# Constant tables made behind the first piece of the decay on VectorE

## The chip, the cores and the metric

The kernel runs on one core of a Trainium2 chip. The metric is device time in microseconds of one launch; the median of the runs shown is used. Five in-order instruction streams matter here: PE (TensorE matmuls, with weight loads shown as PEld), DVE (VectorE), ACT (ScalarE), POOL (GpSimd) and SP (SyncE, which issues nearly all transfers of the stretch in question).

## The reference, cut to what matters

Three layers run one after the other on four batches of 576 tokens.

```python
# attention, 32 heads of 64: causal, with a decay bias from running sums of s
cum  = np.cumsum(np.maximum(s, 0.0), axis=-1)
bias = -(cum[:, :, :, None] - cum[:, :, None, :])
scores = np.where(causal, -1e9, scale * q @ k.T + np.minimum(bias, 0.0))
attn = softmax(scores); x = attn @ v
# gated layer: 512 -> 1024 -> 1024 -> 512
x = (((x @ w1) * (x @ w2)) @ w3) @ w_out
# soft mixture of experts, 32 slots
logits = x @ phi
slot_input = softmax(logits, axis=0).T @ x
slot_out   = relu(slot_input @ w1[e]) @ w2[e]
out = softmax(logits, axis=1) @ slot_out
```

## The kernel before

**Attention.** There are 40 items: for the first eight heads, tokens 0 to 319 (items 0 to 7) and tokens 320 to 575 (items 8 to 15) are items of their own, later heads are one item each. An item's scores (`att_scores`, line 359) are matmuls over 68 rows: 64 of q or k and 4 *decay rows*, which hold the running sum of s and its rounding remainder. So no score of an item can start before its decay rows are in its `raw` tile. DVE takes the maximum (362), ACT the exponential (367), POOL normalises (380), PE transposes (395 for whole tiles, 409 for the diagonal ones), ACT copies the transposed tiles out of PSUM (397, 411), and PE multiplies by v for a pair of heads (`x_ps`), after which ACT and DVE split the result in two parts (444, 445). Transposed tiles go through a PSUM pool named `tp` of two buffers, so a transpose has to wait until the transposed tile two before it was copied out.

**The decay.** `decay_rows` handles the running sums in two pieces of 320 and 256 columns: a clamp (150), a scan (153), a rounded copy (169), its remainder (170), and the two negated (ACT 171, DVE 172). Items 0 and 1 take their decay rows straight from these tiles: four small transfers on SP (322). All others take them from a buffer in DRAM, which three larger transfers on SP fill (176, 177) behind the four and behind two further fetches; item 2 reads it back first (324).

**Weights.** The weights of the gated layer come as 64-bit floats in halves of 128x512 words (`raw_w`, SP line 188, three buffers), and are turned into 32-bit floats by ACT (202) and DVE (205, 206, 209), then split by ACT (233) and POOL (234). These conversions run beside the attention.

**The constant tables.** `masks` (786) makes three small tables from the identity matrix: `rep` (789), `sel4` (791, a copy of rep) and `half` (794). `choice_rows` (957) makes `part` (two reductions on line 962, and line 965). rep is first used by `sum_rows`, sel4 and half in the third layer's steps, part in its last steps.

**What sets the order.** SP issues in the order of the code. The order on PE, DVE, ACT and POOL is set by a scheduler that places instructions by their data and by modelled times. So an instruction that is moved on one engine changes the places of others, on its own engine and on the rest.

Of the kernel before, what the change touches and what calls it, by code (L numbers as in the profile page):

```python
# [11 lines left out]
F32R = mybir.dt.float32r  # L12
# [4 lines left out]
ALU = mybir.AluOpType  # L17
# [30 lines left out]
def attn_glu_softmoe_kernel(  # L48
# [95 lines left out]
    def decay_rows():  # L144
        t0 = dec[0]
        ones = t0[:, 1]
        nc.gpsimd.memset(ones, 1.0)

        def steps(c0, c1):
            nc.vector.tensor_scalar(  # L150
                out=t0[:, 0, c0:c1], in0=t0[:, 0, c0:c1], scalar1=0.0, scalar2=8.0, op0=ALU.max, op1=ALU.mult
            )
            nc.vector.tensor_tensor_scan(
                out=t0[:, 2, c0:c1], data0=ones[:, c0:c1], data1=t0[:, 0, c0:c1],
                initial=t0[:, 2, c0 - 1 : c0] if c0 else 0.0, op0=ALU.mult, op1=ALU.add,
            )

# [6 lines left out]
        for c0, c1 in ((0, 320), (320, 512), (512, S)):  # L164
            if c0 < 512:
                steps(c0, c1 if c1 < 512 else S)
            cum = t0[:, 2, c0:c1]
            p0, p1 = (x[:, :, :, c0:c1] for x in rows) if c1 <= 512 else (rest[:, 0], rest[:, 1])
            nc.vector.tensor_copy(p0[:, 0, 1].bitcast(F32R), cum)
            nc.vector.tensor_tensor(out=p1[:, 0, 1].bitcast(F32R), in0=cum, in1=p0[:, 0, 1], op=ALU.subtract)  # L170
            nc.scalar.activation(out=p0[:, 1, 0], in_=p0[:, 0, 1], func=AF.Copy, scale=-1.0)
            nc.vector.tensor_scalar(out=p1[:, 1, 0], in0=p1[:, 0, 1], scalar1=-1.0, scalar2=None, op0=ALU.mult)

# [583 lines left out]
    with tc.tile_pool(name="att", bufs=1) as ap:  # L757
# [28 lines left out]
        def masks():  # L786

            rep = cp.tile([P, NS], F32, name="rep")
            nc.vector.tensor_reduce(out=rep, in_=ident.rearrange("p (r s) -> p s r", s=NS), axis=AX.X, op=ALU.add)
            sel4 = cp.tile([P, 4, NS], F32, name="sel4")  # L790
            nc.vector.tensor_copy(sel4, rep.unsqueeze(1).broadcast_to([P, 4, NS]))

            half = cp.tile([P, 1], F32, name="half")
            nc.vector.tensor_reduce(out=half, in_=ident[:, :64], axis=AX.X, op=ALU.add)
            return rep, sel4, half
# [162 lines left out]
    def choice_rows():  # L958
        cb = c_all.rearrange("p (b t) s -> p b t s", t=5)

        for k, m in enumerate((8, 16)):
            nc.vector.tensor_reduce(
                out=part[:, k, 0:1], in_=ident.rearrange("p (a r s) -> p a r s", r=2, s=m)[:, :, 1], axis=AX.XY, op=ALU.add
            )
        nc.vector.tensor_scalar(
# [175 lines left out]
```

## Time and profile before

| | us |
|---|---|
| runs | 547.64, 550.87, 552.92 |
| median | 550.87 |
| the profiled execution | 552.43 |
| its span, from first to last instruction | 550.7 |
| mean granted clock of TensorE | 0.993 |

| engine | busy us | share of the span |
|---|---|---|
| PE | 516.8 | 94% |
| DVE | 329.0 | 60% |
| ACT | 311.6 | 57% |
| POOL | 130.6 | 24% |

Busy time is the time in which at least one instruction of the engine was running. The chain that ended last is PE for 70% of the span, transfers for 13%, DVE for 8%. Shares over the whole span say little of one stage: between 200 and 480 us PE hardly ever stands still, and in the first 150 us it waits for a microsecond or less at a time, each time for something else.

### The profile page before, as it was taken

The page shows a single profiled execution, that of the slowest core. Times are in us where ns is not written, and L with a number is a line of the kernel's source. Part 1 is how long each engine was busy: PE and PEld are TensorE (multiplying, and loading weights), DVE is VectorE, ACT ScalarE, POOL GpSimd, SP SyncE. Part 2 cuts the span into 40 slices and gives each one's busy share as a digit, 9 for nine tenths or more (in the row PEclk, how much of TensorE's full clock was granted, in tenths as well). Part 3 has the DMA queues.
Part 4 walks back from the last instruction along what each step waited for, and adds up shares of the span by engine and source line. Part 5 has one row for each costly group of instructions (what it writes and reads, how often), then busy time and mean ns, then how long its engine had stood idle before and what let it go on. Part 6 is the DMA issues. An engine that isn't in the chain of part 4 may idle for free.

```text
span 550.7 us, 11764 instructions
## 1 busy us (share of the span) xinstructions
PE 516.8 (94%) x4288; PEld 434.3 (79%) x4288; DVE 329.0 (60%) x1016; ACT 311.6 (57%) x845; POOL 130.6 (24%) x199
## 2 busy tenths in 40 slices
PE   2799899998999999999999999999999999989993
PEld 2567678877788898999989889899989999843452
DVE  7558787879987394866577668566630311252433
ACT  4567667687986674866577567558644211321222
POOL 4475563102454232110221311111310000000000
PEclk9999989999999999999999999999999999999998
DMA  5746973977673253563656537553514999689977
GB/s 147 235 146 193 280 223 128 292 259 269 218 253 102 73 161 113 169 201 133 194 170 211 173 99 208 176 172 114 167 44 137 413 411 376 241 293 423 420 295 241
DMA packets 38809, 118.03 MB, mean 214 GB/s; under 512 B 4224, under 2 KB 10560, under 8 KB 35296
## 3 DMA queue, kind: packets, MB, share of 16 engines
q1 hardware_dynamic: 36768, 113.60, 61.0%
q10 hardware_dynamic: 1984, 3.69, 2.4%
q8 instruction: 34, 0.56, 0.4%
q14 instruction: 23, 0.19, 0.1%
HBM read 102.11 MB, written 11.60 MB: 206 GB/s over the span
## 4 chain that ended last, share of the span: by engine, by line
PE 70%; DMA 13%; DVE 8%; ACT 4%; issue 2%; POOL 1%; SPq 0%; ACTq 0%; DVEq 0%; POOLq 0%
PE gl L457 31%; PE sc_ps L359 7%; PE x_ps L110 7%; PE pt_ps L395 5%; DMA raw_w<-in_w 5%; PE gn_ps L627 3%; PE o_ps L1042 3%; DMA raw_w3t<-in_w3t 3%; PE h_ps L1004 3%; PE ptd_ps L409 2%; PE z_ps L110 2%; DMA raw_wot<-in_wot 2%; DVE sc L362 1%; PE lg L110 1%; ACT sc L367 1%
## 5 line engine op out<-in xcount | busy, mean ns | idle before, releaser
L457 PE MATMUL gl<-x,w12t 128*128 128x320 f32 (+1 forms) x1536 | 237.7, 304 | 0.1
L457 PEld LDWEIGHTS gl<-x,w12t 128*128 128x128 f32 x1536 | 212.7, 190 | 7.4 <-issue 4.4
L380 POOL TENSOR_SCALAR sc<-sc,rinv 128x64 f32<-128x64 f32 (+4 forms) x160 | 101.1, 650 | 253.0 <-DVE rinv L377 85.7
L367 ACT ACTIVATE sc<-sc,nmax 128x64 f32<-128x64 f32 (+4 forms) x160 | 89.8, 563 | 31.4 <-DVE nmax L362 29.1
L362 DVE CUSTOM_DVE_ANT_0 sc<-sc_ps,mask 128x64 f32<-128x64 f32 (+4 forms) x160 | 65.0, 423 | 31.8 <-PE sc_ps L359 31.0
L397 ACT COPY pt<-pt_ps 128x128 f32<-128x128 f32 (+3 forms) x128 | 53.0, 426 | 34.1 <-PE pt_ps L395 25.1
L395 PE MATMUL pt_ps<-ident,sc 128*128 128x128 f32 x320 | 56.6, 286 | 5.5 <-POOL sc L380 3.2
L395 PEld LDWEIGHTS pt_ps<-ident,sc 128*128 128x128 f32 x320 | 38.4, 144 | 16.9 <-POOL sc L380 7.2
L463 ACT COPY a<-gl 128x256 f32<-128x256 f32 (+1 forms) x64 | 25.4, 398 | 46.0 <-PE gl L457 40.7
L359 PE MATMUL sc_ps<-qa 128*128 128x64 f32 (+1 forms) x144 | 46.4, 334 | 1.3 <-DVE gT L475 0.8
L110 PE MATMUL x_ps<-pt,v 128*64 128x256 f32 (+1 forms) x384 | 47.4, 358 | 0.0
L359 PE MATMUL sc_ps<-raw 68*128 68x288 f32 (+4 forms) x96 | 35.8, 516 | 11.6 <-DMA raw<-rows 9.8
L359 PE MATMUL sc_ps<-qb 68*128 68x64 f32 (+1 forms) x144 | 43.6, 306 | 0.9 <-DMA qb<-qa 0.9
L110 PEld LDWEIGHTS x_ps<-pt,v 128*64 128x64 f32 x384 | 33.5, 140 | 5.8 <-issue 1.0
L359 PEld LDWEIGHTS sc_ps<-raw 68*128 68x128 f32 x96 | 21.6, 265 | 16.9 <-issue 14.1
L202 ACT ACTIVATE w_w<-raw_w 128x512 f32<-128x512 f32 x32 | 21.6, 676 | 17.8 <-DMA raw_w<-in_w 17.7
L445 DVE TENSOR_TENSOR x<-x_ps,x 128x320 fp32r<-128x320 f32 (+1 forms) x32 | 14.1, 452 | 29.2 <-ACT x L444 29.2
L630 ACT COPY gn<-gn_ps 128x512 f32<-128x512 f32 x40 | 22.5, 584 | 15.5 <-PE gn_ps L627 15.1
L367 ACT ACTIVATION_READ_ACCUMULATOR sc<-sc,nmax 128x1 f32 x160 | 30.9, 193 | 0.0
L359 PEld LDWEIGHTS sc_ps<-qa 128*128 128x128 f32 x144 | 27.4, 190 | 3.6 <-DVE gT L475 1.3
L409 PE MATMUL ptd_ps<-ident,sc 128*128 128x128 f32 x160 | 25.9, 286 | 3.2 <-ACT pt L397 3.0
L359 PEld LDWEIGHTS sc_ps<-qb 68*128 68x128 f32 x144 | 27.4, 191 | 1.6 <-DVE v_sb L276 1.0
(180 smaller groups left out, 725.6 us busy)
## 6 DMA issues: line engine op xcount, KB each, us to landing
ew<-in_ew SPq DMA_DIRECT2D x27, 1024.0 KB
raw_w<-in_w SPq DMA_DIRECT2D x32, 512.0 KB
raw<-in_qk SPq DMA_DIRECT2D x24, 576.0 KB
v<-in_v SPq DMA_DIRECT2D x16, 576.0 KB
raw_w3t<-in_w3t SPq DMA_DIRECT2D x16, 512.0 KB
raw_wot<-in_wot SPq DMA_DIRECT2D x8, 512.0 KB
raw_wo<-in_wo SPq DMA_DIRECT2D x8, 512.0 KB
w_d<-w_w SPq DMA_DIRECT2D x8, 512.0 KB
```

Source lines behind the costliest of these rows:

```text
L110: mm = nc.tensor.matmul(out_, lhs, rhs, start=start, stop=stop)
L202: line_up(nc.scalar.activation(out=w, in_=hi.bitcast(F32), func=AF.Copy, scale=F64_SCALE))
L359: nc.tensor.matmul(pp[:r, : z - a], x[:, 0, q0 : q0 + r], x[:, 1, a:z], start=x is mul[0], stop=x is mul[-1])
L362: nc.vector.tensor_tensor_reduce(out=sc[:r, a:z], in0=pp[:r, : z - a], in1=hd["mask"][:r, m0 : m0 + z - a], scale=-0.125, scalar=3.0e38 if ...
L367: nc.scalar.activation(out=sc[:r, :W], in_=sc[:r, :W], func=AF.Exp, bias=nmax[:r, i : i + 1], scale=-1.0, accum_out=rsum[:r, i, 0:1],)
L380: nc.gpsimd.tensor_scalar(out=sc, in0=sc, scalar1=rinv[:, i : i + 1], scalar2=1.0, op0=ALU.mult, op1=ALU.mult)
L395: nc.tensor.transpose(tp[:, j * P : (j + 1) * P], sc[:, j * P : (j + 1) * P], ident)
L397: t["turned", i] = nc.scalar.copy(out=pt[:, p0 : p0 + step * (i - 1) + 1 : step], in_=tp[:, : i * P].rearrange("p (j q) -> p j q", q=P))
L409: nc.tensor.transpose(dg[:, p0 : p0 + P], t["sc"][:, c0 : c0 + P], ident)
L457: nc.tensor.matmul(acc[:, :nt], w12_t[fc][:, wi, n, kc], x_t[b, blk, kc][:, xi], start=k == 0, stop=k == 3 * KC - 1)
L463: st["a_copy"] = nc.scalar.copy(out=a_sb[:, :nt], in_=acc[:, :nt])
L630: st["turned", blk, k, h] = nc.scalar.copy(out=gn[:r, 4 * h : 4 * h + 4].rearrange("p c f -> p (c f)"), in_=tp[:r])
```

## The change

The first instruction of each table on DVE (`rep`, `half`, and the two reductions of `part`) is told to stand behind the last DVE pass of the first piece of the decay (the negation of its remainder, line 172 before, 180 now). It is an order on the same engine, with no semaphore of its own. sel4 and line 965 follow as readers of these. The helper `line`, which wraps the decay passes, only keeps the last step in a list; its loop does nothing.

```diff
+        order = mybir.DependencyInfo(mybir.DependencyClass.NoSync, mybir.DependencyReason.DATA)
+        seq = []
+
+        def line(step):
+            for p in seq:
+                pass
+            seq[:] = [step]
...
-            nc.vector.tensor_scalar(out=p1[:, 1, 0], in0=p1[:, 0, 1], scalar1=-1.0, scalar2=None, op0=ALU.mult)
+            line(nc.vector.tensor_scalar(out=p1[:, 1, 0], in0=p1[:, 0, 1], scalar1=-1.0, scalar2=None, op0=ALU.mult))
+            if not c0:
+                hd["first"] = seq[0]
+
+    def after_first(step):
+        order = mybir.DependencyInfo(mybir.DependencyClass.NoSync, mybir.DependencyReason.DATA)
+        tc.add_manual_dep(step.ins, hd["first"].ins.name, order, reason="order")
...
-            nc.vector.tensor_reduce(out=rep, in_=ident.rearrange("p (r s) -> p s r", s=NS), axis=AX.X, op=ALU.add)
+            after_first(nc.vector.tensor_reduce(out=rep, in_=ident.rearrange("p (r s) -> p s r", s=NS), axis=AX.X, op=ALU.add))
...
-            nc.vector.tensor_reduce(out=half, in_=ident[:, :64], axis=AX.X, op=ALU.add)
+            after_first(nc.vector.tensor_reduce(out=half, in_=ident[:, :64], axis=AX.X, op=ALU.add))
...
-            nc.vector.tensor_reduce(
+            after_first(nc.vector.tensor_reduce(
                 out=part[:, k, 0:1], in_=ident.rearrange("p (a r s) -> p a r s", r=2, s=m)[:, :, 1], axis=AX.XY, op=ALU.add
-            )
+            ))
```

No instruction is added or removed. In the changed kernel, lines of `decay_rows` stand 8 further down and lines behind it 14 further down (359 is 373, 397 is 411, and so on).

DVE at the start of the program, before, from the second clamp of the decay to the pass ahead of line 172 (`dec` is the decay's work tile, `rows_128` and `rows_129` are the tiles that the four small transfers read, `w_w_0_0` is the first half of the weights):

```order
L150 TENSOR_SCALAR dec<-dec 32x256
L789 TENSOR_REDUCE rep<-ident 128x32
L153 SCALAR_TENSOR_TENSOR dec<-dec 32x320
L794 TENSOR_REDUCE half<-ident 128x1
L962 TENSOR_REDUCE part<-ident 128x1 x2
L791 COPY sel_626<-rep 128x128
L169 CAST rows_128<-dec 32x320
L153 SCALAR_TENSOR_TENSOR dec<-dec 32x256
L965 TENSOR_SCALAR part<-part 128x2
L170 TENSOR_TENSOR rows_129<-dec,rows_128 32x320
L169 CAST rows_128<-dec 32x192
L169 CAST rows_130<-dec 32x64
```

The next two rows are a pass over `w_w_0_0` (205) and then line 172 for `rows_129`. The same stretch now:

```order
L158 TENSOR_SCALAR dec<-dec 32x256
L161 SCALAR_TENSOR_TENSOR dec<-dec 32x320
L177 CAST rows_128<-dec 32x320
L161 SCALAR_TENSOR_TENSOR dec<-dec 32x256
L178 TENSOR_TENSOR rows_129<-dec,rows_128 32x320
L177 CAST rows_128<-dec 32x192
L177 CAST rows_130<-dec 32x64
L180 TENSOR_SCALAR rows_129<-rows_129 32x320
L803 TENSOR_REDUCE rep<-ident 128x32
L808 TENSOR_REDUCE half<-ident 128x1
L178 TENSOR_TENSOR rows_129<-dec,rows_128 32x192
```

Six table instructions and the weight pass have gone from ahead of the negation to behind it.

ACT, some 50 instructions in, before (items 4 to 8; `pt_4`, `ptd_4` are the transposed tiles of item 4, `x_0_0_1` is the product with v of items 2 and 3, `w_w12_3_0` and `w_w12_3_1` are the halves of the weight tile 3):

```order
L397 COPY pt_3_369<-pt_ps_3_2_374 128x2x128
L411 COPY ptd_3_370<-ptd_ps_3_378 128x192
L367 ACTIVATE sc_6_453,rsum_1_94<-sc_6_453,nmax_7_515 128x320
L202 ACTIVATE w_w12_3_0_553<-raw_w12_3_0_390 128x512
L397 COPY pt_4_428<-pt_ps_4_1_430 128x128
L444 CAST x_0_0_1_157<-x_ps_2_0_392 128x320
L397 COPY pt_4_428<-pt_ps_4_2_443 128x2x128
L202 ACTIVATE w_w12_3_1_602<-raw_w12_3_1_441 128x512
L367 ACTIVATE sc_8_563,rsum_2_95<-sc_8_563,nmax_8_562 128x448
L411 COPY ptd_4_429<-ptd_ps_4_447 128x192
```

And now:

```order
L216 ACTIVATE w_w12_3_0_553<-raw_w12_3_0_390 128x512
L411 COPY pt_3_369<-pt_ps_3_2_374 128x2x128
L381 ACTIVATE sc_6_453,rsum_1_94<-sc_6_453,nmax_7_515 128x320
L425 COPY ptd_3_370<-ptd_ps_3_378 128x192
L216 ACTIVATE w_w12_3_1_602<-raw_w12_3_1_441 128x512
L247 CAST w12t_3_552<-w_w12_3_0_553 128x512
L381 ACTIVATE sc_8_563,rsum_2_95<-sc_8_563,nmax_8_562 128x448
L381 ACTIVATE sc_8_563,rsum_2_95<-sc_8_563,nmax_8_562 128x576
L247 CAST w12t_3_552<-w_w12_3_1_602 128x512
L411 COPY pt_4_428<-pt_ps_4_1_430 128x128
L458 CAST x_0_0_1_157<-x_ps_2_0_392 128x320
L411 COPY pt_4_428<-pt_ps_4_2_443 128x2x128
```

Both halves of the weight tile 3 and both exponentials of item 8 now stand ahead of the copies of item 4's transposed tiles and of the split of x.

PE at the same place, before:

```order
L359 MATMUL sc_ps_7_2_0_534<-raw_7_312 128x320
L395 MATMUL pt_ps_3_2_374<-ident_86,sc_2_235 128x128 x2
L409 MATMUL ptd_ps_3_378<-ident_86,sc_2_235 128x128 x3
L110 MATMUL x_ps_2_0_392<-ptd_2_329,v_3_250 64x64
L395 MATMUL pt_ps_4_1_430<-ident_86,sc_4_343 128x128
L110 MATMUL x_ps_2_0_392<-ptd_3_370,v_3_250 64x64
```

And now:

```order
L373 MATMUL sc_ps_7_2_0_534<-raw_7_312 128x320
L409 MATMUL pt_ps_3_2_374<-ident_86,sc_2_235 128x128 x2
L423 MATMUL ptd_ps_3_378<-ident_86,sc_2_235 128x128 x3
L373 MATMUL sc_ps_8_3_0_564<-raw_8_362 128x448
L373 MATMUL sc_ps_8_4_0_574<-raw_8_362 128x288
L373 MATMUL sc_ps_8_4_1_577<-raw_8_362 128x288
L409 MATMUL pt_ps_4_1_430<-ident_86,sc_4_343 128x128
L110 MATMUL x_ps_2_0_392<-ptd_2_329,v_3_250 64x64
L110 MATMUL x_ps_2_0_392<-ptd_3_370,v_3_250 64x64
```

Item 8's scores, which stood behind this x_ps and the next transposes, now stand ahead of it. Earlier on PE, the three diagonal transposes of item 0 (409, `ptd_ps`) have moved from ahead of item 2's scores to behind them. Behind the first quarter of the program, PE, POOL and SP stand as before.

## Rows read from the trace of the kernel before

**Rows 1.** Busy time by stretch: PE, PEld, DVE, ACT, POOL, clock, transfer share, GB/s.
```profile
20.00:30.00 10.00, 10.00 (x31) 7.72 (x31) 5.09 (x25) 4.85 (x17) 5.11 (x8) 1.00 0.89 257
...
72.00:90.00 18.00, 16.81 (x97) 14.03 (x93) 16.40 (x37) 15.05 (x34) 10.41 (x8) 0.91 0.56 179
...
200.00:480.00 280.00, 279.62 (x2348) 258.27 (x2348) 151.61 (x480) 155.89 (x430) 47.54 (x85) 1.00 0.58 194
```

**Rows 2.** Chain that ended last, 40 to 64 us: start, length, engine, tile, line.
```profile
39.97 0.43 PE pt_ps L395 x2
...
43.96 0.62 PE pt_ps L395 x2
...
55.86 7.06 DMA raw_w<-in_w
```

**Rows 3.** Chain that ended last, first 20 us.
```profile
4.11 0.28 DVE rep L789
...
5.12 0.11 DVE half L794
5.23 0.26 DVE part L962 x2
5.49 0.13 DVE sel L791
...
6.51 0.06 DVE part L965
...
6.97 0.27 DVE rows L169 x2
...
7.50 0.31 DVE rows L172
```

**Rows 4.** Timeline of SP, first 10 us: start, length, queue, line, transfer, count.
```profile
6.45 3.39 SPq L322 DMA_DIRECT2D raw<-rows  x4
...
7.88 0.65 SPq L322 DMA_DIRECT2D raw<-rows  x1
```

**Rows 5.** Timeline, first 32 us; in brackets idle before, and what ended it.
```profile
9.79 4.61 PE L359 MATMUL sc_ps<-raw 68*128 68x64 f32 x12 [9.79 <-DMA raw<-rows]
...
11.30 0.83 SPq L176 DMA_DIRECT2D rows_d<-rows  x2
...
17.79 0.90 PE L409 MATMUL ptd_ps<-ident,sc 128*128 128x128 f32 x3 [1.28 <-ACT pt L397]
```

**Rows 6.** Share of the transfer engines in tenths, 0 to 10 us, 40 slices.
```profile
DMA  0000000849798998976997868753321100000000
```

**Rows 7.** Timeline of PE, 30 to 60 us.
```profile
31.93 0.37 PE L110 MATMUL x_ps<-ptd,v 128*64 128x64 f32 x1 [0.85 <-ACT ptd L411]
...
44.37 2.10 PE L359 MATMUL sc_ps<-raw 68*128 68x448 f32 x6
...
47.52 1.96 PE L359 MATMUL sc_ps<-raw 68*128 68x448 f32 x6 [0.61 <-DVE w_w L205]
```

**Rows 8.** Share of the transfer engines in tenths, 30 to 50 us, 40 slices.
```profile
DMA  0000000000478379696986986420027777899999
```

**Rows 9.** Timeline of ACT, 36 to 70 us.
```profile
44.88 0.68 ACT L202 ACTIVATE w_w<-raw_w 128x512 f32<-128x512 f32 x1
...
47.13 0.26 ACT L397 COPY pt<-pt_ps 128x128 f32<-128x128 f32 x1
47.29 0.63 ACT L233 CAST w12t<-w_w 128x512 fp32r<-128x512 f32 x1
```

**Rows 10.** Timeline of DVE, 36 to 70 us.
```profile
46.09 0.69 DVE L209 SCALAR_TENSOR_TENSOR w_w<-raw_w,w_w 128x512 uint32<-128x512 uint32 x1
46.69 0.45 DVE L362 CUSTOM_DVE_ANT_0 sc<-sc_ps,mask 128x288 f32<-128x288 f32 x1
...
48.57 1.65 DVE L209 SCALAR_TENSOR_TENSOR w_w<-raw_w,w_w 128x512 uint32<-128x512 uint32 x1
```

**Rows 11.** Timeline of SP, 36 to 110 us.
```profile
45.97 0.52 SPq L188 DMA_DIRECT2D raw_w<-in_w  x1
```

More of the change, by code (lines that the diff above doesn't have):

```diff
@@ L147, in decay_rows @@
         nc.gpsimd.memset(ones, 1.0)
+        order = mybir.DependencyInfo(mybir.DependencyClass.NoSync, mybir.DependencyReason.DATA)
[4 more added lines that the diff above has]
+            seq[:] = [step]
         def steps(c0, c1):
-            nc.vector.tensor_scalar(
+            line(nc.vector.tensor_scalar(
                 out=t0[:, 0, c0:c1], in0=t0[:, 0, c0:c1], scalar1=0.0, scalar2=8.0, op0=ALU.max, op1=ALU.mult
-            )
-            nc.vector.tensor_tensor_scan(
+            ))
+            line(nc.vector.tensor_tensor_scan(
                 out=t0[:, 2, c0:c1], data0=ones[:, c0:c1], data1=t0[:, 0, c0:c1],
                 initial=t0[:, 2, c0 - 1 : c0] if c0 else 0.0, op0=ALU.mult, op1=ALU.add,
-            )
+            ))
         rows = [wp.tile([NH, 2, 2, 512], F32, tag="W", name=f"rows_{a}", bufs=NW) for a in range(2)]
@@ L168, in decay_rows @@
             p0, p1 = (x[:, :, :, c0:c1] for x in rows) if c1 <= 512 else (rest[:, 0], rest[:, 1])
-            nc.vector.tensor_copy(p0[:, 0, 1].bitcast(F32R), cum)
-            nc.vector.tensor_tensor(out=p1[:, 0, 1].bitcast(F32R), in0=cum, in1=p0[:, 0, 1], op=ALU.subtract)
+            line(nc.vector.tensor_copy(p0[:, 0, 1].bitcast(F32R), cum))
+            line(nc.vector.tensor_tensor(out=p1[:, 0, 1].bitcast(F32R), in0=cum, in1=p0[:, 0, 1], op=ALU.subtract))
             nc.scalar.activation(out=p0[:, 1, 0], in_=p0[:, 0, 1], func=AF.Copy, scale=-1.0)
-            nc.vector.tensor_scalar(out=p1[:, 1, 0], in0=p1[:, 0, 1], scalar1=-1.0, scalar2=None, op0=ALU.mult)
+            line(nc.vector.tensor_scalar(out=p1[:, 1, 0], in0=p1[:, 0, 1], scalar1=-1.0, scalar2=None, op0=ALU.mult))
[4 more added lines that the diff above has]
+        tc.add_manual_dep(step.ins, hd["first"].ins.name, order, reason="order")
     def decay_store():
@@ L961, in choice_rows @@
         for k, m in enumerate((8, 16)):
-            nc.vector.tensor_reduce(
+            after_first(nc.vector.tensor_reduce(
                 out=part[:, k, 0:1], in_=ident.rearrange("p (a r s) -> p a r s", r=2, s=m)[:, :, 1], axis=AX.XY, op=ALU.add
-            )
+            ))
         nc.vector.tensor_scalar(
```

## The prediction, made before the changed kernel ran

> **What bounds the kernel now.** I read the busy time by stretches first: it shows which engine has no slack, and where. From 200 to 480 us PE is busy for 279.62 of 280 us [rows 1]. Its work there is fixed, so whatever PE gains or loses before 200 us arrives at the end nearly one for one, as long as nothing after it starts to wait. The question is then what the change does to PE's waits in the first stage. The chain of waits shows that stage as one of many short links: the decay passes on DVE until the first scores, PE afterwards, and from 55.86 us on the fetches of the weights [rows 2]. The timeline of PE shows its holes one by one, and the share of the transfer engines tells when a fetch must have landed.
>
> The table instructions lie on the chain. Between the second clamp of the decay and the negation of the first remainder (line 172) it counts rep 0.28, half 0.11, part 0.26, sel4 0.13 and line 965 0.06, in sum 0.84 us; and from the end of the copies of line 169 at 6.97 + 0.27 = 7.24 to line 172 at 7.50 there are 0.26 us more, for the weight pass that also moves [rows 3]. What waits for line 172 is the second of the four small transfers: line 172 ends at 7.81, the transfer is issued at 7.88, and SP is then busy with issuing up to 9.84 [rows 4]. The first scores start at 9.79, when the decay rows have come [rows 5].
>
> **The change, part by part.** *The front.* All of 0.84 + 0.26 = 1.10 us goes from ahead of line 172. Against it stands one pair of passes, the scan and its copy, that now follow each other directly; I take 0.05 for it, about the size of the smallest piece above. So line 172 should end 1.05 us sooner, at 6.76, the second small transfer be issued at 6.83 and the first scores start at 8.74. Behind the second small transfer SP issues without a gap, so the store to DRAM that is now issued at 11.30 [rows 5] also moves by 1.05, to 10.25. Its other condition, the last negation, is met earlier: even with tables and the weight pass in front of it, everything on DVE up to there is the same set of passes as before. Item 2 and all that follow hang on this store. The instructions that were moved cost nothing where they go: DVE passes the same work before the store is issued, and the tables' first readers come much later.
>
> The small transfers could gain less. The transfer engines are busy with the first weights and the first q and k until about 8.0 us (the 32nd of 40 slices is the last with a share) [rows 6]. If the rows only move after that, they land as long after 8.0 as now after the issue's end, 9.79 - 8.53 = 1.26, so at 9.3, and the first scores gain 0.5. [...] I take 1.05 for the chain as a whole, since the store is bound by SP's issuing and not by this landing; 0.5 is kept as the end of the range.
>
> *The diagonal transposes of item 0.* They took 0.90 us in a hole that PE had anyway, from 17.79 [rows 5]. Now they stand behind item 2's scores, in a stretch where PE is busy for 10.00 of 10 us [rows 1]. That would be 0.90 lost, but the same stretch ends in a wait of 0.85 us for ACT at 31.93 [rows 7], which is as long, so I take 0.05 and keep 0.90 as the bound. To here PE is 1.0 us ahead.
>
> *The order at 39 to 52 us.* This is the term that decides. Before, PE ends item 7's scores at 39.97 and needs until 43.96 + 0.62 = 44.58 for the transposes of item 3, x_ps and the transposes of item 4 [rows 2]; item 8's scores then take it to 44.37 + 2.10 = 46.47 [rows 7]. Now item 8's scores come first. PE starts at 38.97, has 4.61 + 1.89 = 6.50 us of work, and arrives at item 4's diagonal transposes at 45.5. These need a buffer of `tp`, so the copy of item 4's first tile by ACT. That copy now stands behind both conversions of the weight tile 3. The second half's words have landed when the transfer engines fall silent, at about 43.2 (slices of 0.5 us from 30 on) [rows 8], so now at about 42.2. From there: ACT's pass 0.68 [rows 9]; on DVE two passes of the maximum and three of the conversion, which took from 46.69 to 48.57 + 1.65 = 50.22, so 3.53 us, or 2.57 if the last of them takes 0.69 as it did at 46.09 [rows 10]; then the split and the copy on ACT, 47.13 to 47.92, so 0.79 [rows 9]. The copy ends at 42.2 + 0.68 + 0.79 + 2.57 to 3.53, at 46.2 to 47.2. PE waits 0.7 to 1.7 us; the long pass is the exception among the two shown, so I take 1.2, and allow 2.1, since the next transposes wait for the next copies. Against it the wait of 0.61 before item 9's scores [rows 7] goes, since item 8's maxima are long done by then. The net loss is 0.6, between 0.1 and 1.5.
>
> *The rest.* Up to about 100 us some instructions change places by one or two; I set these at nothing: instructions that swap with a neighbour delay one what they bring forward for the other, and PE, POOL and SP keep their order soon after. The cover for it is thin (from 72 to 90 us DVE is busy for 16.40 of 18 us, ACT for 15.05 [rows 1]); if it fails, the price is that of the second rival.
>
> **The sum.** -1.05 + 0.05 + 0.6 = -0.4 us against the profiled execution of 552.43, whose span is 550.7. That gives 552.0 there. The median of the runs is 550.87, 1.56 below the profiled execution, so the forecast in the measure of the median is **550.5 us**. With all ends in its favour the sum is -1.05 + 0.1 = -0.95; with all against it, -0.5 + 0.9 + 1.5 = +1.9.
>
> **The rivals.**
> *The gain arrives whole.* If the words of weight tile 3 land a microsecond or two sooner than the silence of the transfer engines tells (it only gives the latest time), or PE makes up the new hole from the next ones, -1.0 remains: 549.9 us. For it speaks that one fetch need not be the last to land; against it, that the conversion on DVE alone is 2.57 us at best.
> *The weights come late.* The mechanism that ends slower: SP issues in the order of the code, and the fetch of v, which waits for the buffer that x_ps frees, stands ahead of the next weight fetch at 45.97 [rows 11]. PE now ends that x_ps at 45.5 - 0.62 = 44.9 instead of 43.96, so this fetch goes out 0.9 later. Its words are wanted by ACT in front of item 9's last exponential, and the fetches that follow are on the chain, the first with 7.06 us [rows 2]. If the delay of 0.9 is passed on and ACT stands still for as long once more, PE loses 0.9 + 0.9 on top of the forecast: 552.3 us. It decides from the point where the conversion of weight tile 4 waits for its words by more than 1 us. Against it: tile 3 is converted earlier than before, so ACT and DVE have room when the words come.
> *The front gains little.* The small rows stay behind the first weights, and the store too lands no earlier: the order at 39 to 52 us then costs its 0.6 without a gain, 551.5 us.
> [...]
>
> **How the numbers follow.** Forecast 0.38, gain whole 0.25, weights late 0.20, front gains little 0.08, clock 0.09. One per cent of 550.87 is 5.5 us, about what a measurement of this kernel can tell from no change: its three runs alone are 5.3 apart. No case comes near that by itself; only a case plus the spread of runs does. From the two fast cases I get 0.34 times about 0.1, and a little for orders that I did not follow: faster 0.05. From the late weights 0.20 times 0.15, and the same little: slower 0.04. The rest, 0.91, is within. The cases lie between 549.0 and 552.3; a median can be 2 us off on either side by the spread of the runs, which is what sets the width: 547.2 to 553.6.
>
> **What would show each step right or wrong.** The first scores should start at 8.74 (9.3 if the rows queue), the store be issued at 10.25, and item 2's scores start about 1 us sooner than before. The wait of ACT's making before x_ps at 31.93 should be gone or nearly so. Item 4's diagonal transposes should be preceded by a wait of PE for ACT's copy of 0.7 to 1.7 us at about 46, and the next v and weight fetches be issued 0.9 later than before. At 60 us PE should be within 1 us of where it was. The prediction is wrong if the wait at 46 is missing (then the gain should be whole), if PE falls behind by 2 us or more between 52 and 110 us, where I followed no instruction, or if the change moves the time by over 5 us either way, for which I see no place.

## The result, and the profile after

The changed kernel is slower: 557.33 us median (556.06 to 562.65, six runs) against 550.29 (547.64 to 552.92, six runs), ratio 1.0142 with the interval 1.0107 to 1.0178. The forecast was 550.5. Ratios and intervals, here and in the experiments, leave out the executions over 1.5% above the fastest of their kernel (one of e2, two of e15, two of the kernel before); medians and ranges are of all. The profiled execution took 556.26 us, with a span of 554.5 and a mean granted clock of 0.994.

The front did what the prediction said, in this execution at the low end of its range. Timeline of the changed kernel, first 34 us (lines have moved by 8 and 14, as told above):

```profile
5.90 2.99 SPq L336 DMA_DIRECT2D raw<-rows  x4
...
6.54 0.31 DVE L180 TENSOR_SCALAR rows<-rows 32x320 f32<-32x320 f32 x1
...
9.30 4.60 PE L373 MATMUL sc_ps<-raw 68*128 68x64 f32 x12 [9.30 <-DMA raw<-rows]
...
10.35 0.84 SPq L190 DMA_DIRECT2D rows_d<-rows  x2
...
30.98 0.37 PE L110 MATMUL x_ps<-ptd,v 128*64 128x64 f32 x1
```

The negation ends at 6.85 (predicted 6.76), the first scores start 0.49 sooner, the store is issued 0.95 sooner, and the products at 30.98 come 0.95 sooner and without the wait of 0.85 that stood there [rows 5, 7]. So PE enters the stretch of 39 to 52 us ahead by 0.95, and leaves it three to four behind. Busy time in that stretch (columns as in [rows 1]), of the kernel before:

```profile
40.00:52.00 12.00, 11.29 (x64) 8.52 (x64) 8.86 (x25) 7.74 (x21) 5.09 (x8) 1.00 0.73 214
```

and of the changed one:

```profile
40.00:52.00 12.00, 9.01 (x40) 5.58 (x41) 6.61 (x17) 6.96 (x19) 5.83 (x7) 1.00 0.34 97
```

40 rows of PE in place of 64, every engine but POOL less busy, and the transfer engines at 0.34 instead of 0.73. Something holds all of them. Timeline of PE in the changed kernel:

```profile
39.10 0.85 PE L423 MATMUL ptd_ps<-ident,sc 128*128 128x128 f32 x3
42.04 3.75 PE L373 MATMUL sc_ps<-raw 68*128 68x448 f32 x6 [2.09 <-DMA raw<-rows_d]
...
46.20 1.49 PE L110 MATMUL x_ps<-pt,v 128*64 128x256 f32 x8
...
49.00 0.90 PE L423 MATMUL ptd_ps<-ident,sc 128*128 128x128 f32 x3 [0.25 <-ACT pt L411]
...
50.70 0.49 PE L423 MATMUL ptd_ps<-ident,sc 128*128 128x128 f32 x3
51.47 1.96 PE L373 MATMUL sc_ps<-raw 68*128 68x448 f32 x6 [0.28 <-DMA raw<-rows_d]
```

Two things are to be seen. PE stands idle for 2.09 us ahead of item 8's scores, for the decay rows that SP fetches per item. And the scores then take 3.75 us, where the same products took 2.10 in the kernel before [rows 7]. (They are three products; the trace lists each of them twice, so a row says x6, and "six" below means these rows.) The same form takes 1.96 at 51.47, and the three diagonal transposes go from 0.90 to 0.49 between 49.00 and 50.70. Below, "the lower level" stands for the longer of two such durations of one form and "the higher" for the shorter: TensorE is at the lower level up to about 50 us, and at the higher behind it. The clock column shows 1.00 on both sides and does not tell it; the durations do. That the level is TensorE's clock is the author's reading. For it speaks e4 below, a second execution of this program: there the level rises near 36 us and falls back (the three diagonal transposes take 0.55 at 35.33 and 0.85 at 38.26), and the column shows 0.88 for the first 50 us, where the first profile has 1.00. In the kernel before, the step lies earlier (timeline of PE and SP):

```profile
40.19 0.85 PE L409 MATMUL ptd_ps<-ident,sc 128*128 128x128 f32 x3
...
42.05 1.49 PE L110 MATMUL x_ps<-pt,v 128*64 128x256 f32 x7
...
43.99 0.33 SPq L308 DMA_DIRECT2D v<-in_v  x1
...
46.31 0.49 PE L409 MATMUL ptd_ps<-ident,sc 128*128 128x128 f32 x3
```

There the products of items 2 and 3 come first, at the lower level (1.49 for the seven rows at 42.05, which take 0.82 in e12), and item 8's scores mostly behind the rise (2.10, with 0.49 for the diagonal transposes behind them). What sets the level, these two profiles do not tell; e9 to e12 below ask it.

The other half is on ACT, DVE, POOL and SP, whose timelines in the changed kernel read:

```profile
36.12 0.33 SPq L338 DMA_DIRECT2D raw<-rows_d  x1
...
41.52 0.66 ACT L216 ACTIVATE w_w<-raw_w 128x512 f32<-128x512 f32 x1 [2.64 <-DMA raw_w<-in_w]
...
43.40 0.69 DVE L223 SCALAR_TENSOR_TENSOR w_w<-raw_w,w_w 128x512 uint32<-128x512 uint32 x1
43.71 0.67 ACT L216 ACTIVATE w_w<-raw_w 128x512 f32<-128x512 f32 x1 [0.51 <-DMA raw_w<-in_w]
...
46.31 1.27 POOL L248 TENSOR_TENSOR w12t<-w_w,w12t 128x512 fp32r<-128x512 f32 x1
...
46.38 1.75 DVE L223 SCALAR_TENSOR_TENSOR w_w<-raw_w,w_w 128x512 uint32<-128x512 uint32 x1
...
48.16 0.62 ACT L247 CAST w12t<-w_w 128x512 fp32r<-128x512 f32 x1 [0.80 <-DVE w_w L223]
...
48.17 0.33 SPq L322 DMA_DIRECT2D v<-in_v  x1
...
48.69 0.26 ACT L411 COPY pt<-pt_ps 128x128 f32<-128x128 f32 x1
```

ACT stands 2.64 us for the words of weight tile 3 with a copy of item 3 behind it, and the copy of item 4's first tile (48.69) stands behind both conversions. The products of items 2 and 3 end 4.2 us later than before, so the v fetch that needs their buffer goes out at 48.17 instead of 43.99, and SP issues nothing in between. The share of the transfer engines from 30 to 50 us, in the slices of [rows 8], shows the silence:

```profile
DMA  0000000086745797999999931001000000000066
```

From 52 us on, the distance of the two traces at SP's v fetches is 2.9 (55.62 against 52.76), 1.8 near 109 us, and 3.8 at the end.

### The profile page after: what moved, and what is told of

It is laid out like the page before. It is cut to its first block, busy times and chain, and to the rows that moved or that the text cites. A ratio compares the mean times of both kernels' runs of the same rounds, so it can differ in the third digit from the quotient of the medians.

```text
span 554.5 us, 11762 instructions
## 1 busy us (share of the span) xinstructions
PE 517.8 (93%) x4288; PEld 433.8 (78%) x4288; DVE 331.4 (60%) x1016; ACT 311.7 (56%) x845; POOL 129.5 (23%) x199
## 4 chain that ended last, share of the span: by engine, by line
PE 49%; DMA 3%; DVE 2%; ACT 1%; issue 1%; ACTq 0%; SPq 0%; DVEq 0%
PE gl L471 23%; PE x_ps L110 4%; PE sc_ps L373 3%; PE o_ps L1056 3%; PE h_ps L1018 3%; PE pt_ps L409 3%; PE gn_ps L641 2%; PE z_ps L110 1%; DMA raw<-in_qk 1%; PE ptd_ps L423 1%; DMA raw_w<-in_w 1%; PE y_ps L942 1%; PE lg L110 1%; DMA out<-ot 1%; PE out_ps L1080 1%
## 5 line engine op out<-in xcount | busy, mean ns | idle before, releaser
L394 POOL TENSOR_SCALAR sc<-sc,rinv 128x64 f32<-128x64 f32 (+4 forms) x160 | 99.6, 642 | 253.9 <-DVE rinv L391 78.4
L373 PE MATMUL sc_ps<-raw 68*128 68x288 f32 (+4 forms) x96 | 38.5, 542 | 14.5 <-DMA raw<-rows 9.3
L248 POOL TENSOR_TENSOR w12t<-w_w,w12t 128x512 fp32r<-128x512 f32 x16 | 23.1, 1446 | 23.8 <-ACT w12t L247 17.4
```

What stands on the lines that cost most here:

```text
L248: nc.gpsimd.tensor_tensor(out=tl, in0=w, in1=th.bitcast(F32), op=ALU.subtract)
L373: nc.tensor.matmul(pp[:r, : z - a], x[:, 0, q0 : q0 + r], x[:, 1, a:z], start=x is mul[0], stop=x is mul[-1])
L394: nc.gpsimd.tensor_scalar(out=sc, in0=sc, scalar1=rinv[:, i : i + 1], scalar2=1.0, op0=ALU.mult, op1=ALU.mult)
```

## The experiments

The scheduler gave the changed kernel another order on PE, ACT, DVE and POOL, over the first 190 instructions of PE and 150 of DVE; behind them the orders are the same. Nearly all experiments fix the whole order of the four engines by a table, with an order and no semaphore between neighbours on one engine:

```diff
+    while places:
+        n, places = places[0], places[1:]
+        line, places = places[:n], places[n:]
+        for p, k in zip(line, line[1:]):
+            tc.add_manual_dep(nc.get_inst_by_name(f"I-{k}"), f"I-{p}", after, reason="order")
```

In their diffs, - and + rows are pieces of that order. All results in one table; "v fetch" is the one behind the products of items 2 and 3, "scores" the start and length of item 8's six score products, both from the profiled execution. These two columns are single executions: the two of the changed program (changed and e4) are 1.9 us apart in the first of them, and a profile can lie well off the median of its kernel (e7 3.9 over it, e13 2.5 under). So a difference of 2 us there shows nothing by itself.

| kernel | median us | ratio to before, interval | v fetch | scores |
|---|---|---|---|---|
| before | 550.0 to 550.6 | | 43.99 | 44.37, 2.10 |
| changed | 557.33 | 1.0142, 1.0107 to 1.0178 | 48.17 | 42.04, 3.75 |
| e1 tables alone late | 549.47 | 0.9988, 0.9963 to 1.0013 | 41.23 | 41.40, 1.89 |
| e2 the order alone | 559.72 | 1.0140, 1.0099 to 1.0180 | 47.54 | 41.41, 3.75 |
| e3 PE's order back | 563.76 | 1.0237, 1.0203 to 1.0270 | 46.89 | 47.27, 3.62 |
| e4 changed, again | 558.62 | 1.0153, 1.0126 to 1.0179 | 46.31 | 40.18, 3.75 |
| e5 second part back | 551.52 | 1.0016, 0.9989 to 1.0044 | 42.53 | 42.91, 2.20 |
| e6 second part only | 553.90 | 1.0094, 1.0055 to 1.0133 | 45.08 | 39.01, 3.75 |
| e7 first part back | 555.83 | 1.0096, 1.0064 to 1.0129 | 45.55 | 39.42, 3.75 |
| e8 second part back, not PE | 556.35 | 1.0106, 1.0061 to 1.0152 | 46.02 | 39.90, 3.75 |
| e9 fill | 558.30 | 1.0150, 1.0109 to 1.0191 | 46.11 | 42.42, 2.39 |
| e10 fill, wide | 557.17 | 1.0125, 1.0096 to 1.0155 | 46.38 | 43.03, 2.05 |
| e11 early products | 550.88 | 1.0019, 0.9987 to 1.0050 | 41.88 | 42.26, 2.04 |
| e12 early products and fill | 550.17 | 1.0006, 0.9978 to 1.0033 | 40.70 | 40.87, 1.89 |
| e13 e8 with fill | 556.85 | 1.0121, 1.0086 to 1.0157 | 43.97 | 40.71, 1.96 |
| e14 tile 3 later | 555.90 | 1.0112, 1.0067 to 1.0157 | 47.05 | 40.93, 3.75 |
| e15 tile 3 later, with fill | 555.68 | 1.0059, 1.0023 to 1.0094 | 44.46 | 41.07, 2.09 |

### The move, or the order that came with it (e1 to e4)

**e1** takes the order of before, and of the change only the first 22 instructions of DVE and 6 of ACT:

```diff
-L789 TENSOR_REDUCE rep<-ident 128x32
-L794 TENSOR_REDUCE half<-ident 128x1
 ...
 L172 TENSOR_SCALAR rows_129<-rows_129 32x320
+L789 TENSOR_REDUCE rep<-ident 128x32
+L794 TENSOR_REDUCE half<-ident 128x1
```

> The tables and the first weight pass stand behind line 180 as in the change, ACT's first six rows too; every other row on PE, ACT, DVE and POOL has its place of before. Theory (the order that the scheduler made behind the front costs the time, not the move of the tables): the gain of the front alone, first scores at about 9.3, store at about 10.35, 0.5 to 1.0 us faster than before, some 549.5 us. Rival (the moved tables themselves hold something up): slower than before by 4 us or more, 554 to 558.

**e2** is the opposite: tables as before, everything behind them in the changed kernel's order.

```diff
 L789 TENSOR_REDUCE rep<-ident 128x32
 ...
+L359 MATMUL sc_ps_2_0_0<-raw_2
 L409 MATMUL ptd_ps_0<-ident,sc_0
-L359 MATMUL sc_ps_2_0_0<-raw_2
 ...
```

> The counterpart: the tables stand where they stood before, and everything behind the front has the order of the changed kernel. Theory (order): the loss without the gain, 4 to 8 us slower than before, 554 to 558 us, with PE standing before item 8's scores at about 43 us. Rival (tables): within 1 us of before.

**e3** is the changed kernel with PE's order of before, ACT, DVE and POOL as changed:

```diff
-L373 MATMUL sc_ps_8_3_0<-raw_8
 L110 MATMUL x_ps_2_0<-ptd_2,v_3
 ...
+L373 MATMUL sc_ps_8_3_0<-raw_8
```

> The changed kernel with PE's order of before (68 of 3440 rows), ACT, DVE and POOL as changed. Theory A (item 8's scores ahead of x_ps on PE are the cause, since they wait there for their decay rows): PE's wait of 2.1 us at 42 goes, most of the loss goes, 549 to 552 us. Theory B (ACT's conversions of weight tile 3 ahead of the copies are the cause, since they wait for words): ACT still stands 2.6 us for the words at about 39 to 41.5, item 3's copies and x_ps are held behind it, and 554 us or more remain.

**e4** is the changed kernel without an edit.

> The changed kernel once more, for a second profile. Theory (order): about 3 us behind the kernel before at 60 us, as in the first profile, since the order is the same; what lies beyond, from 3.8 in the profiled pair to 7 in the medians, must come from later, where the order is that of before: from the granted clock or from run spread. Rival: a larger loss in the first 60 us in this execution, 6 us or more.

e1 is 0.9988, e2 1.0140: the move of the tables is worth at most 2 us and shows none of it for certain, and a fixed order costs nothing that can be measured (e1 has one: 0.9963 to 1.0013); the order behind the tables carries the whole loss (e2 lies above the 554 to 558 expected). That PE's order is the only cause fell with e3, which came out as theory B had it and is the slowest of all. There PE has its products of items 2 and 3 first again and waits for ACT, which still has the words of weight tile 3 ahead of the copies. Timelines of PE and ACT in e3:

```profile
42.94 0.66 ACT L216 ACTIVATE w_w<-raw_w 128x512 f32<-128x512 f32 x1 [2.80 <-DMA raw_w<-in_w]
...
44.00 0.45 PE L409 MATMUL pt_ps<-ident,sc 128*128 128x128 f32 x1 [2.37 <-ACT pt L411]
...
53.10 0.90 PE L423 MATMUL ptd_ps<-ident,sc 128*128 128x128 f32 x3 [2.21 <-ACT pt L411]
```

e4 was 4.3 us behind the kernel before at 60 us (the v fetch at 64.60), where 3 were expected. Timelines of PE and SP in e4:

```profile
47.97 0.90 PE L423 MATMUL ptd_ps<-ident,sc 128*128 128x128 f32 x3 [1.08 <-ACT pt L411]
...
50.52 3.62 PE L373 MATMUL sc_ps<-raw 68*128 68x448 f32 x6
...
58.11 0.33 SPq L322 DMA_DIRECT2D v<-in_v  x1
```

Here PE does wait for the copy of item 4's first tile, item 9's scores are at the lower level too (3.62; 1.96 at 51.47 in the first profile), and the next v fetch goes out 5.4 behind the kernel before (58.11 against 52.76) in place of 2.9. The first profile is the mild case. Item 9's scores take 1.96 in the profiles of before, e1, e5, e11 and e12, which lose nothing that can be measured, and 3.23 to 3.75 in those of e2, e3, e4, e6 to e10 and e15. Only three profiles of kernels that lose have 1.96, those of the changed kernel, e13 and e14, and each of the three is faster than the median of its kernel. So a second stretch at the lower level, behind 49 us, is probably a part of the 7.0 that the first profile does not show.

### The place (e5 to e8)

**e5** is the changed kernel with the order of before in a second part alone, on four engines; **e6** puts the changed order into that part of e1 alone; **e7** puts the part ahead of it back (all rows up to PE's 58th), and leaves the second as changed; **e8** is e5 without PE. The diff of e5, for PE and ACT (e6 has it with the signs turned; e7's rows are the pieces ahead of it, such as the diagonal transposes of item 0 ahead of item 2's scores; e8 has only the second fence and its like on DVE and POOL):

```diff
-L373 MATMUL sc_ps_8_3_0<-raw_8, sc_ps_8_4_0, sc_ps_8_4_1
 L110 MATMUL x_ps_2_0<-ptd_2,v_3, and the rest of this product
 L409 MATMUL pt_ps_4_2<-ident,sc_4
+L373 MATMUL sc_ps_8_3_0<-raw_8, sc_ps_8_4_0, sc_ps_8_4_1
```

```diff
-L216 ACTIVATE w_w12_3_1<-raw_w12_3_1
-L247 CAST w12t_3<-w_w12_3_0
-L381 ACTIVATE sc_8<-sc_8,nmax_8, twice
-L247 CAST w12t_3<-w_w12_3_1
 L411 COPY pt_4<-pt_ps_4_1
 L458 CAST x_0_0_1<-x_ps_2_0
 L411 COPY pt_4<-pt_ps_4_2
+L216 ACTIVATE w_w12_3_1<-raw_w12_3_1
+L381 ACTIVATE sc_8<-sc_8,nmax_8
```

> The changed kernel, with the order of before in the second part alone (item 8's scores to item 6's first transposes, weight tiles 3 and 4: PE rows 58 to 93, ACT 50 to 71, DVE 77 to 100, POOL 48 to 49 of the order), all four engines. Theory 'second part' (the 4.2 us are lost there, and the rest only carries them on): the v fetch that stood at 48.17 in the changed kernel is issued at 43 to 44, and the time is 549 to 552. Rival 'arrival' (the front that is early sends fetches into queues that are full, so that item 8's rows land late whatever the order): the v fetch at 46 or later, 555 to 558. Rival 'third part' (the order behind 52 us costs as much again): v fetch at 43 to 44, but 553 to 556 at the end.

> The kernel whose tables alone are late (all else in the order of before), with the changed kernel's order put into the second part alone, on the four engines. Theory 'second part': the v fetch of items 2 and 3 at 45 to 48 in place of 41.2, and 554 to 558. Rivals 'arrival' and 'third part': 549 to 552.

> The changed kernel with the order of before in the first part alone (all rows ahead of the second part, other than the tables and decay passes themselves). Theory 'second part': 554 to 558, the v fetch at 45 to 48. Rival 'first part' (the items' order ahead of 39 us makes the rows and weights late, and the second part only shows it): 549 to 552, with the v fetch at 41 to 44.

> The changed kernel with the order of before in the second part on ACT, DVE and POOL, and PE's as changed (item 8's scores ahead of the products of items 2 and 3). Theory 'conversions' (ACT and DVE stand at weight tile 3's words ahead of copies that PE waits for): 549 to 552, the v fetch at 43 to 45. Rival 'scores first' (PE's own place for item 8's scores is what costs, ACT's wait is beside it): 554 to 558, PE idle some 2 us ahead of item 8's scores and the v fetch at 46 or later. Rival 'match' (the orders of the engines only fit together): 558 or more.

The second part holds it: with it back (e5) the loss is gone within the interval, although the first part and the part behind 52 us keep the changed order; alone (e6) it costs 0.94%; with the first part back (e7) 0.96% stay. That the rows are late whatever the order fell too: PE waits 0.49 for them in e6 and 0.23 in e8, and both lose (e6 at the lower edge of what was expected of it). e8 came out as "scores first" had it, though without the idle 2 us. Timelines of PE and ACT in e8:

```profile
39.90 3.75 PE L373 MATMUL sc_ps<-raw 68*128 68x448 f32 x6 [0.23 <-DMA raw<-rows_d]
...
45.64 0.27 ACT L411 COPY pt<-pt_ps 128x128 f32<-128x128 f32 x1 [4.46 <-PE x_ps L110]
...
48.72 0.41 PE L409 MATMUL pt_ps<-ident,sc 128*128 128x128 f32 x2 [1.30 <-ACT ptd L425]
...
51.95 2.21 PE L471 MATMUL gl<-x,w12t 128*128 128x320 f32 x6
```

Item 8's scores at the lower level stand ahead of the products that ACT and SP wait for; ACT's order of before cannot use the time (4.46 us idle); then PE waits for ACT, and at 51.95 it is at the lower level again (2.21 where the kernel before has 1.12). e5 has none of this:

```profile
42.91 2.20 PE L373 MATMUL sc_ps<-raw 68*128 68x448 f32 x6
44.95 0.49 PE L423 MATMUL ptd_ps<-ident,sc 128*128 128x128 f32 x3
...
48.04 1.12 PE L471 MATMUL gl<-x,w12t 128*128 128x320 f32 x6
```

### The clock alone (e9 to e12)

Extra products of the identity with itself, into unused columns of a PSUM bank, read by nobody, change what PE does without moving anything else. **e9** puts five of them into the changed kernel's idle 2.09 us, **e10** four there and four behind item 2's diagonal transposes. **e11** puts twenty into e1 ahead of the first scores, **e12** adds four behind the diagonal transposes of items 0 to 3.

```diff
+    EARLY, FILL = 0, {3: 5}          # e10: 0, {2: 4, 3: 4}; e11: 20, {}; e12: 20, {0: 4, 1: 4, 2: 4, 3: 4}
+
+    def fill(tile, c0, n):
+        for _ in range(n):
+            nc.tensor.matmul(tile[:, c0 : c0 + P], ident, ident, start=True, stop=True)
...
+            if n == 0 and i == tiles[0] and m == 0:
+                fill(pp, 3 * P, EARLY)
...
+            fill(dg, 3 * P, FILL.get(n, 0))
             t["turned", "d"] = nc.scalar.copy(
```

> The changed kernel with five extra products of the identity with itself (128x128, f32, into unused columns of the bank of item 3's diagonal transposes, read by nobody) between those transposes and item 8's scores, where PE stood idle for 2.09 us. Every other instruction keeps its place. Theory 'clock level' (the 4 us are PE at half its clock for longer: item 8's six score products take 3.75 us where the kernel before has 2.10, because the stretch without work and the scores come where the kernel before has the products of items 2 and 3, behind which its clock rose): the clock rises 3 to 8 us earlier than near 49.8, item 8's scores or the products behind them take half, 553 to 556. Rival 'waits' (the rows' and weights' waits in front of the queues are the 4 us): nothing changes or it loses up to 0.5 us, 557 to 559.

> As the run before it, with four such products behind item 2's diagonal transposes and four behind item 3's: 3.4 us of extra work at the lower clock, of which the idle 2.1 us hide a part. Theory 'clock level': PE has no stretch without work from 35 to 43, the clock rises before item 8's scores end, 552 to 556. Rival 'waits': 1.3 us of the extra work comes on top, 558 to 560.

> The kernel whose tables alone are late (all else in the order of before) with twenty extra products of the identity with itself ahead of the first scores, while PE has nothing to do (3 to 9 us). Theory 'clock level': PE is at its higher clock when the first twelve score products start (2.3 us where they take 4.61), falls back when the work that follows thins out, and the gain is 0 to 2 us: 547.5 to 550. Rival (the level is not set by what PE did just before): twelve products 4.6 us, 549 to 551.

> The same with four more extra products behind the diagonal transposes of each of items 0 to 3. Theory 'clock level': it holds the higher level for longer ahead of 41 us, or rises again sooner; every us at the higher level gives back up to half a us, and each extra product costs 0.43 us at the lower level and 0.21 at the higher: between 544 (held throughout) and 555 (held nowhere, 16 x 0.43 us on top). Rival 'waits': 552 to 556.

Timelines of PE and ACT in e9:

```profile
40.29 2.34 PE L404 MATMUL ptd_ps<-ident 128*128 128x128 f32 x10
42.42 2.39 PE L375 MATMUL sc_ps<-raw 68*128 68x448 f32 x6
...
49.20 0.26 ACT L419 COPY pt<-pt_ps 128x128 f32<-128x128 f32 x1
...
49.51 0.55 PE L431 MATMUL ptd_ps<-ident,sc 128*128 128x128 f32 x3 [3.08 <-ACT pt L419]
...
54.72 2.21 PE L480 MATMUL gl<-x,w12t 128*128 128x320 f32 x6
```

The clock did rise ahead of the end of item 8's scores (2.39, where both profiles of the changed program have 3.75), and nothing was gained: 558.30, as the rival "waits" had it. The v fetch is 2.1 sooner than in the first profile of the changed kernel, but 0.2 sooner than in e4. PE arrives early at the copy of item 4's first tile, which ACT makes no sooner than before, waits 3.08 us for it, and falls back to the lower level (2.21 at 54.72). (The trace counts each extra product twice.) That the level at item 8's scores is the only cause fell with this. e10, at 557.17, lies between what the two theories expected, and not apart from the change itself. In e11 and e12 the higher level is bought for the front. First scores and the first wait behind them, in e1, on which both are built:

```profile
8.82 4.61 PE L359 MATMUL sc_ps<-raw 68*128 68x64 f32 x12 [8.82 <-DMA raw<-rows]
14.98 0.47 PE L395 MATMUL pt_ps<-ident,sc 128*128 128x128 f32 x1 [1.55 <-POOL sc L380]
```

and in e11:

```profile
9.86 2.52 PE L361 MATMUL sc_ps<-raw 68*128 68x64 f32 x12
15.91 0.47 PE L403 MATMUL pt_ps<-ident,sc 128*128 128x128 f32 x1 [3.53 <-POOL sc L382]
...
18.07 3.88 PE L361 MATMUL sc_ps<-raw 68*128 68x64 f32 x10
```

The scores take 2.52 instead of 4.61, so the rival that the level does not follow from what PE did just before is out. But they start 1.04 later than in e1, because the extra products still run (from 2.45 to 10.02), and PE hands the rest to a longer wait for POOL: the transposes behind them come at 15.91, 0.93 later than in e1; then the level falls (3.88 for the ten products at 18.07, 2.00 in e12). e11 lies just above what the clock theory expected, and its interval meets that of e1. In e12 the higher level holds for longer (the ten products at 19.85 take 2.00, 3.54 in the kernel before), and its median is that of before too. By these two, a higher level in the front gives nothing back, since PE then waits for POOL (3.53 in e11, 3.54 in e12; 1.55 in e1); a start of the scores at the higher level without the delay of 1.04 was not tried.

### Both together (e13 to e15)

**e13** is e8 with the fill of e9. **e14** leaves PE's order as changed and puts only the conversion passes of weight tile 3 later; **e15** is e14 with the fill. The diff of e14 on ACT (the second `w12t_3` cast follows two copies further on; on DVE the last pass of the first half and the three of the second stand behind item 8's maxima):

```diff
-L216 ACTIVATE w_w12_3_0<-raw_w12_3_0
 L411 COPY pt_3<-pt_ps_3_2
 L381 ACTIVATE sc_6<-sc_6,nmax_7
 L425 COPY ptd_3<-ptd_ps_3
-L216 ACTIVATE w_w12_3_1<-raw_w12_3_1
-L247 CAST w12t_3<-w_w12_3_0
+L216 ACTIVATE w_w12_3_0<-raw_w12_3_0
 L381 ACTIVATE sc_8<-sc_8,nmax_8, twice
-L247 CAST w12t_3<-w_w12_3_1
 L411 COPY pt_4<-pt_ps_4_1
 L458 CAST x_0_0_1<-x_ps_2_0
 L411 COPY pt_4<-pt_ps_4_2
+L216 ACTIVATE w_w12_3_1<-raw_w12_3_1
 L425 COPY ptd_4<-ptd_ps_4
+L247 CAST w12t_3<-w_w12_3_0
```

> The changed kernel with the order of before in the second part on ACT, DVE and POOL (as e8), and the five extra products ahead of item 8's scores (as e9). Theory 'both' (each of clock and copies hides the other): the clock rises near 43, no wait of more than 1.3 us for a copy follows, 550 to 553. Rival 'match' (ACT's order of before cannot go with PE's scores first, since ACT stands at the copy of item 4 until the products end): v fetch near 46 and 555 to 557 as e8.

> The changed kernel, in which only the conversion passes of weight tile 3 on ACT, DVE and POOL are put behind item 8's maxima and exponentials and behind the copies of items 4 and 5's first transposes. Theory 'copies': PE has no wait for copies from 48 to 51 and the time is 553 to 555. Theory 'both': the idle 2.09 us and the lower level stay, 555 to 557. Rival 'rows' (the late rows alone): 557.

> The same with the five extra products ahead of item 8's scores. Theory 'both': the clock rises near 43, the wait of 3.08 us that e9 had for a copy is gone, the second diagonal transposes end near 48, 551 to 554. Rival 'match': 556 or more.

The conversions later alone give 1.0112, as "both" expected, with an interval that meets that of the change; the fill alone 1.0150; the two 1.0059. e15 lies between what "both" and "match" expected of it. Its interval does not meet that of e9 or of the change, and by it over half of the loss goes when the clock and the copies are both seen to. But its interval meets that of e14, and the median of its twelve executions, 555.68, is close to that of e14 (555.90). So e15 points to a gain and does not settle its size, and that the fill adds to the later conversions is not shown. The rest is still there, in e15 as waits and a fall of the clock:

```profile
46.08 0.55 PE L431 MATMUL ptd_ps<-ident,sc 128*128 128x128 f32 x3 [1.30 <-ACT pt L419]
...
48.76 3.62 PE L375 MATMUL sc_ps<-raw 68*128 68x448 f32 x6
```

e13's median went against "both" (550 to 553 expected, 556.85 measured) and is the one that "match" expected. Its profile does not show why: its v fetch goes out at 43.97, as in the kernel before, where "match" expected 46, its scores of items 8 and 9 both take 1.96, and at 60 us it is 0.1 behind the kernel before. That execution, at 554.31 the fastest of the six, loses its time behind 60 us. What holds e13 is open. No version here is faster than the kernel before; e1, e5, e11 and e12 are not told apart from it.

## Why the prediction was wrong

**The front** was right in its mechanism. In the first profile it is 0.49 at the first scores, 0.95 at the store and 0.95 at 31 us. Of the thirteen profiles with the tables moved and no extra products ahead of the first scores, eight have these at 8.82 to 8.87, close to the predicted 8.74, and five at 9.00 to 9.69; the 9.3 kept for rows that queue (9.30 in the first profile) is met in some executions and not in most. What it is worth at the end is open: e1 lies 0.7 us below before, with an interval from -2.0 to +0.7.

**The diagonal transposes of item 0** were right: the wait behind them took them up [rows 7], and e5, which keeps that place as changed, loses nothing that can be measured.

**The order at 39 to 52 us** is the step that failed. It said a net loss of 0.6, 1.5 at most, and PE at item 4's diagonal transposes at 45.5. In the first profile PE goes from 0.95 ahead to 4.2 behind by the v fetch, so the term measures 5.1 there. PE was ready for the transposes at 49.00 - 0.25 = 48.75, 3.25 late, by two things (3.95 together; the rest of its work was some 0.7 shorter than the prediction had it):
- Of the 6.50 us of work, 1.89 are item 8's scores, taken from a row of 2.10 that lies behind the rise of the clock [rows 7]. The step puts these products ahead of the rise, where they take 3.75: 1.86 more. The two durations of one form in the same trace were there to be seen, 0.85 and 0.49 for the three diagonal transposes.
- Item 8's scores were taken to start when PE is free. Their decay rows, issued at 36.12 behind weights and q and k, came at 42.0, 2.09 after PE was free. In the kernel before, these scores start at 44.37 without a wait [rows 7]. This wait differs between executions (1.08 in e4, the same program) and is not what decides (e8 waits 0.23 and still loses).

The copy of item 4's first tile was given for 46.2 to 47.2 and ended at 48.69 + 0.26 = 48.95. The second half's words, given for 42.2 by the silence of the transfer engines, came at 43.71, and the second conversion ahead of the copy waits for DVE's last pass, which took 1.75 beside a pass of POOL and ended at 48.13, behind the maxima of item 8's late scores. The predicted wait of 0.7 to 1.7 us for the copy is therefore not in the first profile (0.25), which the prediction would have read as "the gain is whole". It is 1.08 in e4, and more where PE is made early (3.08 in e9, 1.30 in e15).

**The rival "weights come late"** had the late v fetch right and its size and its reason wrong. It put the fetch 0.9 later and 1.8 us on the whole; the fetch went out 4.2 later, and the transfer engines stood silent for it. But its own condition, a wait of more than 1 us for the words of weight tile 4, is not met. Timeline of ACT in the changed kernel:

```profile
54.46 0.69 ACT L216 ACTIVATE w_w<-raw_w 128x512 f32<-128x512 f32 x1 [0.47 <-DMA raw_w<-in_w]
...
56.81 0.67 ACT L216 ACTIVATE w_w<-raw_w 128x512 f32<-128x512 f32 x1 [0.74 <-DMA raw_w<-in_w]
```

The measured loss is 7.0. Of this, 3.8 are between the spans of the two profiled executions; that of before is 2.1 over the median of its kernel, and that of the change 1.1 under.

**The rest, at nothing**, held: e5 has the changed order ahead of and behind the second part, and is at 1.0016.

**The clock** column shows a dip at 72 to 90 us in the kernel before (0.91) [rows 1]. In the changed kernel it is not there (1.00), and another stands at 52 to 72 (0.91); the profiles of e1, e5 and e7 have 1.00 and 1.00, 0.91 and 1.00, 1.00 and 0.81 in the two stretches. The 549.0 at the low end of the prediction's cases, with its chance of 0.09, lies 1.5 us under the forecast, as much as 0.09 of the 16.81 busy us of that stretch [rows 1] (an estimate). No run shows this term: the changed kernel lost 7.0, and e1, whose profile has no dip from 50 to 100 us, is at 0.9988. The mean clocks are not the same in all kernels: over the executions the mean granted clock is 0.989 to 0.993 in before, e1 and e5, and 0.975 to 0.989 in the kernels that lose. Within the kernels, an execution with a clock lower by 0.01 is some 2 us longer (an estimate, a straight line through the executions' distances from the means of their kernels). So a part of the loss may go with a lower clock behind the first rise. But e11 and e12, at 0.969 and 0.978, lose nothing, and whether a lower clock causes waits or follows from them is open. The level ahead of 50 us, which the clock column does not show (1.00 for 0 to 50 in both first profiles), entered no term of the prediction.

What stays open is how the loss divides. The second part as a whole, on four engines, is shown to carry it (e5, e6, e7). PE's order changed with the others put back (e8) costs, and so do the others' changed orders with PE's put back (e3), so the orders have no separate prices that add up. That the clock level and ACT's copies are what passes the loss on is read from the profiles; no run takes both away and shows the loss gone.

## What to carry to other kernels

A small edit under a scheduler is judged by the order that comes out, on all engines, and here it did not help to put it back on some engines alone: e3 and e8, each with a half of the old order, are both slower than the kernel before, and e3 is slower than the change itself. A duration that was carried from one place in a trace to another was 1.86 us short here, because the level was not the same (1.89 taken, 3.75 measured), so compare one form of product on both sides first: the clock column showed 1.00 on both. On ACT here, a pass that waited 2.64 us for its words held the copy of item 3 behind it as well; to move the conversions alone (e14) gained nothing that can be told apart. And one profile is one execution: a second one of the same program (e4) had another wait, another level and 1.9 us less at the fetch that the first was read by.

## What had not been expected of the hardware

In the profiled executions of before and of the change TensorE ran the first 44 to 50 us at its lower level, although the profile of before has it busy for 10.00 of 10 us from 20 to 30 [rows 1], and it rose during or soon behind the products with v (the three diagonal transposes take 0.85 at 40.19 and 0.49 at 46.31 in before, 0.90 at 49.00 and 0.49 at 50.70 in the change); in e9, behind the fill (item 8's scores take 2.39 at 42.42). Two executions of one program differ in it: e4 had item 7's scores (six rows) in 1.32 us and fell back, the changed kernel above has 2.48 for them at 36.40.

```profile
36.48 1.32 PE L373 MATMUL sc_ps<-raw 68*128 68x64 f32 x6 [0.16 <-DVE nmax L376]
...
40.18 3.75 PE L373 MATMUL sc_ps<-raw 68*128 68x448 f32 x6 [1.08 <-DMA raw<-rows_d]
```

One DVE pass of a single form (L223, 128x512) took 0.69 and 1.75 us three microseconds apart in the changed kernel (43.40 and 46.38). The traces tell what goes with it: the second runs beside a conversion pass of POOL (46.31), the first beside none. Of the 32 passes of this form in the first 150 us of the profiles of before and of the change, the 13 with no POOL instruction beside them took 0.67 to 0.69; the others are longer by about 0.86 us for each us that a conversion pass of POOL runs beside them (an estimate, a straight line through all 32). In the kernel before, the pass of 1.65 us at 48.57 [rows 10] runs beside such a pass too, so the long pass that the prediction kept as a possibility goes with that neighbour.
